# Four full-width partial sums moved from VectorE to accumulating DMAs, with the order of all steps rebuilt

## The chip, the cores and the metric

The kernel runs on one core of a Trainium2 chip. The time is the device time of one execution in microseconds (us), from the core's first instruction to its last, plus some 1.7 us that lie around the span which the profile shows (143.15 against 141.4 in the profiled run before). Every kernel is run several times, and the kernel before is run beside it on the same chip. Runs that lie over 1.5% above the fastest run of the same kernel are called slow and are left out of all comparisons.

## The reference, cut to what matters

Two independent halves work on 2048 positions of width 448 and are written side by side.

```python
def _A_ref(x, ...):                       # a state-space layer
    Bu = einsum("bld,pd->blp", x, B_bar)  # complex
    for t in range(L):
        h = Lam_bar * h + Bu[:, t, :]     # a scan over 2048 positions
    y = 2.0 * einsum("blp,dp->bld", hseq, Cmat).real + x * Dskip

def _B_ref(x, wqkv, wo):                  # local attention, 16 heads of 28
    q, k, v = ...                         # x @ wqkv
    idx = pos[:, None] - arange(8) * 2    # 8 keys per query, 2 apart
    attn = softmax(where(idx >= 0, q . k[idx] * scale, -1e9))
    o = sum over w of attn[..., w] * v[idx[..., w]]
    return o @ wo
```

The change concerns the sum over the eight window places `w` in half B. Half A shares all the engines with it.

## The kernel before

TensorE computes the projections, the scan of half A as matmuls over chunks, and the outputs. VectorE computes the eight products of the attention sum for each of four groups of four positions (a "quad": 0, 4, 8, 12), and most of the adds. (In the prediction and the expectations the quads are also counted from 0 to 3: "quad 2" there is quad 8 here, "quad 1" is quad 4.) Some adds are made by DMA: GpSimd issues a transfer from SBUF to SBUF that adds what it carries to what lies at its goal.

```python
def pv_m(self, j0, w):                    # step u.j.w: one product, on VectorE        (L325)
    ...
    self.nc.vector.tensor_tensor(self.pv_buf(j0, w), self.at[...]..., self.vd[...], op=ALU.mult)

def pv_a(self, j0, w, i0=0, i1=4):        # step d.j.w: accumulator += product w       (L330)
    acc = self.pv_buf(j0, 0)[:, i0:i1]
    self.nc.vector.tensor_tensor(acc, acc, self.pv_buf(j0, w)[:, i0:i1], op=ALU.add)

def pv_f(self, j0, w):                    # step f.j.w: product w += product w+1, DMA  (L334)
    a_, b_ = (self.pv_buf(j0, w + i)... for i in (0, 1))
    self.nc.gpsimd.dma_start(a_, b_, accum_op=ALU.add)
```

`pv_buf(j0, 0)` is the accumulator `pvb`, so `f.j.0` adds the product of w = 1 into the accumulator itself; the other products lie in `pvt`. Each such transfer carries 448 KB. A finished quad is turned by a transposing DMA (`tu`, oT<-pvb, L338) for the output product with `wo`. Half A loads its input by transposing DMAs and writes its output tile by tile:

```python
def load_x(self, a, b):                   # step X.a.b, two transposing DMAs           (L418, L419)
    self.nc.sync.dma_start_transpose(out=self.xT[:, b, 0:3, a, :], in_=...)
    self.nc.sync.dma_start_transpose(out=self.xT[:, b, 3, a, :], in_=...)

def y_e(self, a, b, eng):                 # step y.a.b: evict one output tile, store it
    ya = self.pool.tile([NCH, D], bf16, name="ya", tag="ya", bufs=3)
    self.cx.ev(eng, ya[:], self.ps_t["y", a, b][:])                 # PSUM to SBUF     (L83)
    self.nc.sync.dma_start(self.out_a[:, 4 * a + b, :], ya[:])      #                  (L717)
```

There are three tiles of `ya`: the fourth eviction must wait until the first store has landed. All transposing DMAs and stores are issued by SyncE (`SPq` in the page's list of issues), one after the other. The instruction order of every engine is fixed by one long table, read step by step: `L` local states of half A, `C`/`c` their corrections and evictions, `Y`/`y` half A's outputs, `O`/`o`/`od` half B's outputs, and so on; the last letter of an eviction, which copies a finished tile out of PSUM, where the matmuls write, names its engine (A ScalarE, V VectorE).

Of the kernel before, what the change touches and what calls it, by code (L numbers as in the profile page):

```python
# [16 lines left out]
S = 2048  # L17
D = 448
T = 16
# [4 lines left out]
H = 16  # L24
# [696 lines left out]
def body(ctx: ExitStack, tc: tile.TileContext, A_x, A_Lre, A_Lim, A_Bre, A_Bim, A_Cre, A_Cim, A_logdt, A_Dskip,  # L721
# [27 lines left out]


ORDER = """
    lw P.0.1.1.0.3 pp P.0.0.0.0.3 P.0.0.1.0.3 P.0.0.1.3.4 P.0.1.1.3.4 P.0.2.1 p.0.0.1.A p.0.1.1.A P.0.0.0.3.4 xa
    X.3.2 p.0.0.0.A P.0.1.0.0.3 P.0.1.0.3.4 p.0.2.1.A p.0.1.0.A P.0.2.0 p.0.2.0.A X.0.0 P.0.3.0 p.0.3.0.A
    P.1.1.1 p.1.1.1.A P.2.2.0 p.2.2.0.A P.2.1.1 p.2.1.1.A pe tb X.0.1 P.1.2.0 R.0.0.1.2 R.0.1.1.2 P.1.1.0
    p.1.1.0.A P.2.1.0 P.1.0.0 p.2.1.0.A tb tb p.1.2.0.A R.0.1.2.3 P.1.0.1 p.1.0.1.A P.1.3.0 p.1.3.0.A R.0.0.2.3
    R.0.0.0.1 S.0.0 T.0 St.0.0 R.0.1.0.1 S.0.1 St.0.1 s.0.A V.14 P.3.1.1 p.3.1.1.A p.1.0.0.A P.3.2.0 Z tb pg
    mt.0 mr.0 T.1 p.3.2.0.A sk mb.0.V P.1.2.1 p.1.2.1.A R.1.0 V.8 v.8.A X.1.1 P.2.0.1 P.2.2.1 p.2.0.1.A
    p.2.2.1.A V.9 v.9.A P.3.1.0 P.2.0.0 p.2.0.0.A p.3.1.0.A P.2.3.0 X.3.1 X.3.0 B.0 p.2.3.0.A X.2.0 P.3.0.1 ms.0
    X.1.0 me.0 B.6 R.1.1 S.1.0 St.1.0 b.6.A S.1.1 b.0.A St.1.1 P.3.0.0 p.3.0.0.A p.3.0.1.V B.3 V.13 X.1.3 b.3.A
    P.3.2.1 v.14.A s.1.A lc V.3 R.2.0 V.11 mt.1 p.3.2.1.A T.2 v.11.A R.2.1 B.1 mr.1 mb.1.A V.10 v.10.A S.2.0  # L760
    St.2.0 S.2.1 St.2.1 v.13.A s.2.A v.3.A X.2.2 V.15 P.3.3.0 R.3.0 p.3.3.0.A mt.2 V.5 V.0 R.3.1 v.15.A X.2.1
    V.2 ms.1 T.3 V.12 V.6 B.2 b.1.A v.0.A S.3.0 St.3.0 S.3.1 pa me.1 v.2.V v.12.A v.5.A St.3.1 s.3.A mr.2 mb.2.V
    X.1.2 ms.2 V.1 v.1.A v.6.A mt.3 M.1.V H.10.14 V.4 b.2.A V.7 M.2.V mr.3 me.2 mb.3.V M.4.V ms.3 M.0.V L.0.0
    B.4 M.3.V L.0.1 al me.3 l.0.0.A l.0.1.A N.0 n.0 L.0.3 l.0.3.A b.4.A X.2.3 v.7.A H.6.10 N.3 n.3 u.0.0 v.4.A
    B.5 L.1.1 l.1.1.A u.0.1 L.1.0 l.1.0.A N.15 n.15 b.5.A L.0.2 u.0.3 l.0.2.A X.0.2 L.1.3 L.2.6 l.2.6.A L.2.4
    u.0.2 L.2.2 l.2.4.A d.0.1 N.12 u.0.4 H.0.6 L.0.5 n.12 l.0.5.A L.2.1 l.2.1.A u.0.5 u.0.7 N.9 n.9 L.2.0 L.0.6
    l.1.3.A l.0.6.A l.2.0.A X.3.3 N.6 n.6 L.0.4 u.4.0 l.2.2.A l.0.4.A X.0.3 L.2.3 L.1.2 l.1.2.A L.3.2 f.0.2
    l.2.3.A L.3.3 l.3.2.A L.3.0 sa d.0.2 L.3.1 l.3.3.A l.3.0.A u.0.6 L.1.6 f.0.4 u.4.1 l.3.1.A sc la.0 L.1.4
    l.1.6.A u.4.2 u.4.3 d.4.1 d.0.4 L.1.5 le.0 ro.0 l.1.4.A u.4.5 l.1.5.A f.0.6 d.0.6 L.2.5 l.2.5.A L.3.6 sm
    sn.0 f.4.2 L.3.4 l.3.4.A bk.0 be.0.A u.4.4 f.4.4 d.4.2 l.3.6.A u.4.7 u.4.6 L.3.5 tu.0 G.2.A G.3.A l.3.5.A  # L770
    la.1 g.2.A g.3.A C.1.2.V C.0.2.V O.0.0 o.0.0.A C.1.3.A le.1 c.0.2.V ro.1 O.2.0 o.2.0.A c.1.2.V G.0.A c.1.3.A
    sn.1 f.4.6 u.8.0 C.2.2.A O.2.1 G.1.A bk.1 c.2.2.A g.0.A O.0.1 be.1.A G.5.V d.4.4 u.8.4 g.1.A G.4.V g.4.V
    C.0.1.A c.0.1.A Y.3.3 g.5.V o.0.1.A C.1.0.V d.4.6 tu.4 y.3.3.A c.1.0.V G.6.V g.6.V C.2.3.A c.2.3.A Y.1.3
    u.8.6 u.8.3 C.2.0.V C.0.0.A c.2.0.V u.8.7 Y.2.3 C.1.4.A Y.0.3 o.2.1.A od.2 f.8.6 u.8.2 od.0 c.0.0.A f.8.2
    c.1.4.A y.1.3.A C.2.4.V C.1.5.V y.2.3.A u.8.5 c.2.4.V c.1.5.V O.6.0 C.0.3.V c.0.3.V f.8.4 C.0.5.V O.6.1
    c.0.5.V y.0.3.A o.6.0.A C.0.4.A o.6.1.A od.6 u.8.1 C.0.6.V O.4.1 c.0.6.V C.1.1.V c.0.4.A c.1.1.V C.1.6.V
    O.4.0 C.2.5.V c.2.5.V d.8.1 Y.0.0 y.0.0.A C.2.1.V Y.2.0 Y.3.0 y.3.0.A c.2.1.V y.2.0.A o.4.0.A o.4.1.A od.4
    d.8.2 c.1.6.V C.2.6.V d.8.4 c.2.6.V u.12.2 Y.3.2 Y.2.2 d.8.6 u.12.4 Y.1.1 tu.8 Y.1.0 Y.0.1 y.2.2.A Y.1.2
    u.12.3 y.1.0.A y.0.1.A f.12.2 y.1.1.A O.8.0 o.8.0.A u.12.1 O.8.1 o.8.1.A Y.3.1 O.10.1 y.3.1.A u.12.5 Y.2.1
    u.12.6 f.12.4 y.1.2.A u.12.7 u.12.0 d.12.1 d.12.6 y.3.2.A O.10.0 o.10.0.A d.12.7 d.12.2 d.12.4.0.2 od.8  # L780
    tm.12 Y.0.2 o.10.1.A d.12.4.2.4 tm.14 te.12 O.12.0 O.12.1 od.10 y.0.2.A te.14 o.12.0.A o.12.1.A od.12
    y.2.1.A O.14.0 o.14.0.S O.14.1 o.14.1.S
"""


# [52 lines left out]
```

## Time and profile before

| | before |
|---|---|
| median time | 142.65 us (142.19 to 142.72, 3 runs) |
| TensorE busy | 134.3 us, 95% of the span of 141.4 |
| VectorE busy | 124.0 us, 88% |
| ScalarE, GpSimd busy | 57%, 32% |
| bytes on the queue that carries GpSimd's transfers | 6.65 MB, 26.2% of the time of 16 DMA engines |

The prediction shows the lines on TensorE and VectorE. Here are the DMA engines. The next lines are stretches of the trace of the kernel before: the stretch in us, its length, the busy time of TensorE, its weight loads, VectorE, ScalarE and GpSimd with their instructions, the granted TensorE clock as a share of full speed, the mean busy share of the 16 DMA engines (which goes above 1, here to 1.23), and GB/s.

```profile
66.00:72.00 6.00, 6.00 (x36) 3.18 (x35) 5.93 (x9) 3.38 (x7) 1.81 (x2) 1.00 0.78 134
72.00:78.00 6.00, 6.00 (x30) 2.68 (x29) 5.86 (x8) 3.42 (x7) 0.85 (x1) 1.00 1.23 188
...
84.00:90.00 6.00, 6.00 (x36) 3.12 (x35) 5.96 (x11) 4.54 (x11) 0.85 (x1) 1.00 0.51 96
...
114.00:120.00 6.00, 5.33 (x41) 2.95 (x39) 5.13 (x7) 1.92 (x5) 0.00 (x0) 1.00 0.44 147
120.00:124.00 4.00, 4.00 (x30) 2.25 (x27) 4.00 (x5) 0.99 (x2) 0.86 (x1) 1.00 0.78 158
```

From 66 to 90 us the DMA engines are full (a share of 1 or more) in one stretch of four (72 to 78); 78 to 84, left out, had a share of 0.84. From the list of DMA issues on the page (goal and source, issuer, how many, KB each, median us from issue to landing):

```profile
pvt<-pvt POOLq DMA_DIRECT2D x11, 448.0 KB, 4.7
out_dram<-ya SPq DMA_DIRECT2D x16, 112.0 KB, 3.8
```

### The profile page before, as it was taken

The numbers are of one execution on the slowest core, as the hardware profiler recorded it, in microseconds if no ns is written. First come the engines' busy times: TensorE is split into PE (matmuls) and PEld (weight loads), VectorE is DVE, ScalarE is ACT, GpSimd is POOL, SyncE is SP. The second block draws the span as 40 slices with busy tenths as digits, with TensorE's granted clock in tenths as the row PEclk, the third lists the DMA queues.
The fourth block names the chain that finished last, engine by engine and source line by source line (L and its number), as shares of the span: only waits on it lengthen the run. The fifth ranks groups of instructions, "written<-read, shape, count | busy, mean of one in ns | idle before, by whom it ended". The sixth has DMA issues, their size and how long they took to land. (4 is left out here: it accounts for less than half of the span.)

```text
span 141.4 us, 2554 instructions
## 1 busy us (share of the span) xinstructions
PE 134.3 (95%) x919; PEld 72.1 (51%) x919; DVE 124.0 (88%) x166; ACT 80.4 (57%) x166; POOL 45.0 (32%) x108
## 2 busy tenths in 40 slices
PE   6999999999998999999999999999999998999990
PEld 5244445555564756644544544655554554555540
DVE  0069999999999999999999999999999979999521
ACT  1238998759944947594465447555555123243680
POOL 8279599999940000002112200300024000220000
PEclk9999999999999999999999999999999999999998
DMA  4999898555762244526999956770379963797433
GB/s 108 292 202 197 188 221 112 104 115 114 156 151 49 52 101 121 135 56 175 143 163 196 188 96 130 133 131 0 74 218 214 205 172 130 163 212 178 151 111 134
DMA packets 36426, 20.49 MB, mean 145 GB/s; under 512 B 27762, under 2 KB 34048, under 8 KB 36413
## 3 DMA queue, kind: packets, MB, share of 16 engines
q1 hardware_dynamic: 33214, 13.32, 41.1%
q0 software_dynamic: 2736, 6.65, 26.2%
q10 hardware_dynamic: 463, 0.35, 1.0%
q8 instruction: 7, 0.11, 0.3%
q14 instruction: 6, 0.05, 0.1%
HBM read 3.62 MB, written 3.67 MB: 52 GB/s over the span
## 5 line engine op out<-in xcount | busy, mean ns | idle before, releaser
L325 DVE TENSOR_TENSOR pvt<-attn,vd 128x1792 bf16<-128x1792 bf16 x28 | 29.2, 1082 | 0.0
L600 PE MATMUL u_ps<-xaT,Bcat 128*128 128x512 bf16 x112 | 27.4, 379 | 0.0
L239 DVE TENSOR_TENSOR pr<-qT,kT 128x2048 bf16<-128x2048 bf16 (+1 forms) x12 | 26.9, 2279 | 0.0
L334 POOL DMA_DIRECT2D pvt<-pvt x11 | 9.5, 864 | 51.8 <-DVE pvt L325 51.5
L711 PE MATMUL y_ps<-C,u 128*128 128x448 bf16 x112 | 24.1, 353 | 0.7 <-DVE u L693 0.7
L83 ACT CAST u<-u_ps 128x512 bf16<-128x512 f32 x28 | 16.0, 591 | 12.8 <-PE u_ps L600 6.0
L191 PE MATMUL qk_ps<-xbT,wqkv_nat 128*128 128x512 bf16 x96 | 22.6, 382 | 0.0
L330 DVE TENSOR_TENSOR pvb<-pvb,pvt 128x1792 bf16<-128x1792 bf16 (+1 forms) x18 | 18.4, 1034 | 1.1 <-DMA pvt<-pvt 0.9
L83 ACT CAST ya<-y_ps 128x448 bf16<-128x448 f32 x16 | 8.1, 535 | 15.9 <-PE y_ps L711 11.2
L600 PEld LDWEIGHTS <-Bcat 128*128 128x128 bf16 x112 | 10.6, 98 | 11.2
L191 PEld LDWEIGHTS <-wqkv_nat 128*128 128x128 bf16 x96 | 9.2, 99 | 10.7 <-issue 1.0
L711 PEld LDWEIGHTS <-u 128*128 128x128 bf16 x112 | 9.8, 98 | 8.6 <-DVE u L693 1.1
L216 PE MATMUL v_ps<-wqkv_nat,xbT 128*128 128x448 bf16 x64 | 14.1, 355 | 0.0
L358 PE MATMUL wo_ps<-wo_p,oT 128*128 128x448 bf16 x64 | 14.1, 352 | 0.0
L83 ACT CAST kT<-qk_ps 128x512 bf16<-128x512 f32 (+3 forms) x22 | 9.9, 454 | 3.3 <-PE qk_ps L191 3.1
L83 ACT CAST qT<-qk_ps 128x512 bf16<-128x512 f32 (+1 forms) x20 | 9.4, 495 | 1.8 <-PE qk_ps L191 1.7
L83 ACT CAST yb<-wo_ps 128x448 bf16<-128x448 f32 x14 | 7.3, 537 | 5.4 <-PE wo_ps L358 5.3
L216 PEld LDWEIGHTS <-xbT 128*128 128x128 bf16 x64 | 8.6, 146 | 2.7 <-issue 0.2
L358 PEld LDWEIGHTS <-oT 128*128 128x128 bf16 x64 | 6.2, 98 | 5.9
L693 DVE TENSOR_TENSOR u<-co,u 128x512 bf16<-128x512 f32 x14 | 9.0, 678 | 0.0
L83 ACT CAST vd<-v_ps 128x448 bf16<-128x448 f32 x15 | 7.7, 541 | 1.6 <-PE v_ps L216 1.6
L577 POOL MEMSET Bcat<- 64x128 bf16 x7 | 1.4, 223 | 22.1 <-ACT Bcat L83 22.1
(177 smaller groups left out, 202.8 us busy)
## 6 DMA issues: line engine op xcount, KB each, us to landing
pvt<-pvt POOLq DMA_DIRECT2D x11, 448.0 KB, 4.7
out_dram<-ya SPq DMA_DIRECT2D x16, 112.0 KB, 3.8
out_dram<-yb SPq DMA_DIRECT2D x7, 224.0 KB, 2.2
vd<-vd SPq DMA_DIRECT2D x2, 392.0 KB
wqkv_nat<-in_B_wqkv_dram SPq DMA_DIRECT2D x2, 336.0 KB, 4.3
wo_p<-in_B_wo_dram POOLq DMA_DIRECT2D x16, 42.0 KB, 2.9
vd<-vd SPq DMA_DIRECT2D x1, 588.0 KB
xaT<-in_A_x_dram SPq DMA_TRANSPOSE x32, 3.5
```

The source lines that it names most:

```text
L83: nc.scalar.copy(out, in_)
L191: self.nc.tensor.matmul(self.ps_t[c, g, which][:], lhsT=wv[:, k], rhs=self.xT[:, k, c * CH:(c + 1) * CH], start=(k == 0), stop=(k == KT - 1))
L216: self.nc.tensor.matmul(ps[:], lhsT=xv[:, k, j, :], rhs=self.wn[:, k, 2, :], start=(k == 0), stop=(k == KT - 1))
L239: self.nc.vector.tensor_tensor(pr[:, :, g0:g1, :], self.qT[:, c, g0:g1].unsqueeze(1).to_broadcast([NCH, 4, n, CH]), self.windows(self.kT[: ...
L325: self.nc.vector.tensor_tensor(self.pv_buf(j0, w), self.at[:, w, j0:j0 + 4, :].unsqueeze(2).to_broadcast([NCH, 4, DH, H]), self.vd[:, off: ...
L330: self.nc.vector.tensor_tensor(acc, acc, self.pv_buf(j0, w)[:, i0:i1], op=ALU.add)
L334: self.nc.gpsimd.dma_start(a_, b_, accum_op=ALU.add)
L358: self.nc.tensor.matmul(ps[:], lhsT=oT[:, s + k, :], rhs=self.wo_p[:, KT * n + k, :], start=(k == 0), stop=(k == KT - 1))
L577: self.nc.gpsimd.memset(self.Bcat[0:PL, 3, i, :], 0.0)
L600: nc.tensor.matmul(ps4[:], lhsT=self.Bcat[:, k, m, :], rhs=self.xT[:, b, k], start=(k == 0), stop=(b % 2 == 0 and k == KT - 1))
L693: self.nc.vector.tensor_tensor(h_, ps, h_, op=ALU.add)
L711: nc.tensor.matmul(ps[:], lhsT=self.state(m, a, b), rhs=self.C[:, m, :], start=False, stop=(m == NM - 1), skip_group_check=True)
```

## The change

The intent is to relieve VectorE: in each of the four quads the add of the w = 1 product into the accumulator is done by a DMA, and the whole order is rebuilt around the new waits. No code but the order table differs. Its core, with the rest cut:

```diff
 ORDER = """
-    ... u.0.2 L.2.2 l.2.4.A d.0.1 N.12 u.0.4 H.0.6 ...
-    ... X.3.3 N.6 n.6 L.0.4 u.4.0 l.2.2.A l.0.4.A X.0.3 ...
-    ... l.3.1.A sc la.0 L.1.4 l.1.6.A u.4.2 u.4.3 d.4.1 d.0.4 ...
-    ... O.4.0 C.2.5.V c.2.5.V d.8.1 Y.0.0 y.0.0.A ...
-    ... f.12.4 y.1.2.A u.12.7 u.12.0 d.12.1 d.12.6 ...
+    ... L.0.0 l.0.5.A f.0.2 f.0.0 u.0.5 l.0.2.A L.1.4 L.1.3 l.1.4.A X.0.3 N.6 X.3.3 ...
+    ... d.0.6 L.1.6 l.3.2.A f.4.0 la.0 L.1.5 u.4.4 ...
+    ... f.8.2 tu.4 Y.0.3 u.8.1 f.8.0 C.0.0.V c.0.0.V C.0.4.V ...
+    ... Y.3.0 y.3.0.A y.1.0.A Y.2.0 f.12.0 u.12.3 f.12.2 Y.0.0 ...
     (all other steps: the same set in a new order, but for the engine that finishes 20 tiles:
      nine corrections, five group sums, six other evictions)
```

More of the change, by code (lines that the diff above doesn't have):

```diff
@@ L751 @@
 ORDER = """
-    lw P.0.1.1.0.3 pp P.0.0.0.0.3 P.0.0.1.0.3 P.0.0.1.3.4 P.0.1.1.3.4 P.0.2.1 p.0.0.1.A p.0.1.1.A P.0.0.0.3.4 xa
-    X.3.2 p.0.0.0.A P.0.1.0.0.3 P.0.1.0.3.4 p.0.2.1.A p.0.1.0.A P.0.2.0 p.0.2.0.A X.0.0 P.0.3.0 p.0.3.0.A
-    P.1.1.1 p.1.1.1.A P.2.2.0 p.2.2.0.A P.2.1.1 p.2.1.1.A pe tb X.0.1 P.1.2.0 R.0.0.1.2 R.0.1.1.2 P.1.1.0
-    p.1.1.0.A P.2.1.0 P.1.0.0 p.2.1.0.A tb tb p.1.2.0.A R.0.1.2.3 P.1.0.1 p.1.0.1.A P.1.3.0 p.1.3.0.A R.0.0.2.3
-    R.0.0.0.1 S.0.0 T.0 St.0.0 R.0.1.0.1 S.0.1 St.0.1 s.0.A V.14 P.3.1.1 p.3.1.1.A p.1.0.0.A P.3.2.0 Z tb pg
@@ L757 @@
-    mt.0 mr.0 T.1 p.3.2.0.A sk mb.0.V P.1.2.1 p.1.2.1.A R.1.0 V.8 v.8.A X.1.1 P.2.0.1 P.2.2.1 p.2.0.1.A
-    p.2.2.1.A V.9 v.9.A P.3.1.0 P.2.0.0 p.2.0.0.A p.3.1.0.A P.2.3.0 X.3.1 X.3.0 B.0 p.2.3.0.A X.2.0 P.3.0.1 ms.0
-    X.1.0 me.0 B.6 R.1.1 S.1.0 St.1.0 b.6.A S.1.1 b.0.A St.1.1 P.3.0.0 p.3.0.0.A p.3.0.1.V B.3 V.13 X.1.3 b.3.A
-    P.3.2.1 v.14.A s.1.A lc V.3 R.2.0 V.11 mt.1 p.3.2.1.A T.2 v.11.A R.2.1 B.1 mr.1 mb.1.A V.10 v.10.A S.2.0
-    St.2.0 S.2.1 St.2.1 v.13.A s.2.A v.3.A X.2.2 V.15 P.3.3.0 R.3.0 p.3.3.0.A mt.2 V.5 V.0 R.3.1 v.15.A X.2.1
@@ L762 @@
-    V.2 ms.1 T.3 V.12 V.6 B.2 b.1.A v.0.A S.3.0 St.3.0 S.3.1 pa me.1 v.2.V v.12.A v.5.A St.3.1 s.3.A mr.2 mb.2.V
-    X.1.2 ms.2 V.1 v.1.A v.6.A mt.3 M.1.V H.10.14 V.4 b.2.A V.7 M.2.V mr.3 me.2 mb.3.V M.4.V ms.3 M.0.V L.0.0
-    B.4 M.3.V L.0.1 al me.3 l.0.0.A l.0.1.A N.0 n.0 L.0.3 l.0.3.A b.4.A X.2.3 v.7.A H.6.10 N.3 n.3 u.0.0 v.4.A
-    B.5 L.1.1 l.1.1.A u.0.1 L.1.0 l.1.0.A N.15 n.15 b.5.A L.0.2 u.0.3 l.0.2.A X.0.2 L.1.3 L.2.6 l.2.6.A L.2.4
-    u.0.2 L.2.2 l.2.4.A d.0.1 N.12 u.0.4 H.0.6 L.0.5 n.12 l.0.5.A L.2.1 l.2.1.A u.0.5 u.0.7 N.9 n.9 L.2.0 L.0.6
@@ L767 @@
-    l.1.3.A l.0.6.A l.2.0.A X.3.3 N.6 n.6 L.0.4 u.4.0 l.2.2.A l.0.4.A X.0.3 L.2.3 L.1.2 l.1.2.A L.3.2 f.0.2
-    l.2.3.A L.3.3 l.3.2.A L.3.0 sa d.0.2 L.3.1 l.3.3.A l.3.0.A u.0.6 L.1.6 f.0.4 u.4.1 l.3.1.A sc la.0 L.1.4
-    l.1.6.A u.4.2 u.4.3 d.4.1 d.0.4 L.1.5 le.0 ro.0 l.1.4.A u.4.5 l.1.5.A f.0.6 d.0.6 L.2.5 l.2.5.A L.3.6 sm
-    sn.0 f.4.2 L.3.4 l.3.4.A bk.0 be.0.A u.4.4 f.4.4 d.4.2 l.3.6.A u.4.7 u.4.6 L.3.5 tu.0 G.2.A G.3.A l.3.5.A
-    la.1 g.2.A g.3.A C.1.2.V C.0.2.V O.0.0 o.0.0.A C.1.3.A le.1 c.0.2.V ro.1 O.2.0 o.2.0.A c.1.2.V G.0.A c.1.3.A
@@ L772 @@
-    sn.1 f.4.6 u.8.0 C.2.2.A O.2.1 G.1.A bk.1 c.2.2.A g.0.A O.0.1 be.1.A G.5.V d.4.4 u.8.4 g.1.A G.4.V g.4.V
-    C.0.1.A c.0.1.A Y.3.3 g.5.V o.0.1.A C.1.0.V d.4.6 tu.4 y.3.3.A c.1.0.V G.6.V g.6.V C.2.3.A c.2.3.A Y.1.3
-    u.8.6 u.8.3 C.2.0.V C.0.0.A c.2.0.V u.8.7 Y.2.3 C.1.4.A Y.0.3 o.2.1.A od.2 f.8.6 u.8.2 od.0 c.0.0.A f.8.2
-    c.1.4.A y.1.3.A C.2.4.V C.1.5.V y.2.3.A u.8.5 c.2.4.V c.1.5.V O.6.0 C.0.3.V c.0.3.V f.8.4 C.0.5.V O.6.1
-    c.0.5.V y.0.3.A o.6.0.A C.0.4.A o.6.1.A od.6 u.8.1 C.0.6.V O.4.1 c.0.6.V C.1.1.V c.0.4.A c.1.1.V C.1.6.V
@@ L777 @@
-    O.4.0 C.2.5.V c.2.5.V d.8.1 Y.0.0 y.0.0.A C.2.1.V Y.2.0 Y.3.0 y.3.0.A c.2.1.V y.2.0.A o.4.0.A o.4.1.A od.4
-    d.8.2 c.1.6.V C.2.6.V d.8.4 c.2.6.V u.12.2 Y.3.2 Y.2.2 d.8.6 u.12.4 Y.1.1 tu.8 Y.1.0 Y.0.1 y.2.2.A Y.1.2
-    u.12.3 y.1.0.A y.0.1.A f.12.2 y.1.1.A O.8.0 o.8.0.A u.12.1 O.8.1 o.8.1.A Y.3.1 O.10.1 y.3.1.A u.12.5 Y.2.1
-    u.12.6 f.12.4 y.1.2.A u.12.7 u.12.0 d.12.1 d.12.6 y.3.2.A O.10.0 o.10.0.A d.12.7 d.12.2 d.12.4.0.2 od.8
-    tm.12 Y.0.2 o.10.1.A d.12.4.2.4 tm.14 te.12 O.12.0 O.12.1 od.10 y.0.2.A te.14 o.12.0.A o.12.1.A od.12
@@ L782 @@
-    y.2.1.A O.14.0 o.14.0.S O.14.1 o.14.1.S
+    xa P.0.1.1.0.3 pp P.0.1.0.0.3 P.0.0.0.0.3 P.0.0.0.3.4 p.0.0.0.A P.0.1.0.3.4 P.0.1.1.3.4 p.0.1.0.A
+    P.0.0.1.0.3 X.2.3 X.3.2 P.0.2.0 p.0.1.1.A pe p.0.2.0.A P.0.0.1.3.4 P.1.1.0 X.3.1 P.0.2.1 X.1.0 p.1.1.0.A tb
+    P.1.2.0 X.3.0 p.0.0.1.V R.0.1.0.1 p.0.2.1.A R.0.0.0.1 R.0.0.2.3 P.2.0.1 R.0.0.1.2 p.2.0.1.A P.0.3.0
+    p.1.2.0.A P.1.0.1 p.0.3.0.A p.1.0.1.A X.2.2 P.1.1.1 p.1.1.1.A R.0.1.2.3 P.1.3.0 P.1.2.1 P.3.1.0 lc S.0.0 tb
+    T.0 St.0.0 p.1.2.1.A R.0.1.1.2 S.0.1 p.1.3.0.A St.0.1 s.0.A tb tb P.1.0.0 P.3.0.1 X.0.0 P.2.1.0 pg P.2.0.0
@@ new lines @@
+    p.1.0.0.A T.1 mt.0 mr.0 p.3.0.1.A mb.0.V X.0.2 p.2.0.0.A p.3.1.0.A lw R.1.0 p.2.1.0.A R.1.1 P.2.1.1 P.2.2.0
+    p.2.2.0.A P.2.3.0 p.2.3.0.A V.13 ms.0 B.1 P.2.2.1 p.2.1.1.A B.0 b.1.A p.2.2.1.A Z P.3.3.0 p.3.3.0.A P.3.2.1
+    p.3.2.1.A V.3 v.3.A B.6 b.6.A P.3.2.0 S.1.0 St.1.0 p.3.2.0.A b.0.A S.1.1 St.1.1 s.1.A v.13.A R.2.0 T.2
+    P.3.0.0 p.3.0.0.A V.9 R.2.1 v.9.A P.3.1.1 mt.1 X.2.0 me.0 V.12 v.12.A V.11 mr.1 X.2.1 B.4 p.3.1.1.A V.1
+    S.2.0 R.3.0 St.2.0 S.2.1 St.2.1 V.10 v.1.A mb.1.A ms.1 V.15 v.11.A T.3 V.8 R.3.1 v.15.A s.2.A V.14 mt.2 mr.2
@@ new lines @@
+    mb.2.V v.10.A M.1.V X.1.2 V.5 v.14.A me.1 b.4.A V.6 X.1.1 M.0.V V.7 v.8.A S.3.0 St.3.0 S.3.1 St.3.1 v.7.A
+    s.3.A v.6.A pa v.5.A sk ms.2 H.6.10 V.2 mt.3 me.2 V.4 v.4.A mr.3 mb.3.V v.2.A V.0 ms.3 al L.0.4 me.3 l.0.4.A
+    M.2.V M.3.V v.0.A B.3 N.3 N.0 n.3 B.2 L.2.1 L.2.0 b.3.A n.0 M.4.V H.10.14 u.0.3 L.2.3 l.2.1.A u.0.2 l.2.3.A
+    H.0.6 b.2.A N.12 L.0.3 l.2.0.A N.9 L.0.6 X.0.1 B.5 L.2.4 l.0.3.A L.0.2 b.5.A u.0.1 L.0.5 l.2.4.A u.0.0
+    l.0.6.A n.9 sm L.0.0 l.0.5.A f.0.2 f.0.0 u.0.5 l.0.2.A L.1.4 L.1.3 l.1.4.A X.0.3 N.6 X.3.3 l.1.3.A u.0.7
@@ new lines @@
+    X.1.3 u.0.6 L.1.2 l.0.0.A f.0.6 u.0.4 f.0.4 n.6 L.1.0 l.1.0.A L.0.1 u.8.0 L.2.2 u.4.3 L.3.3 d.0.2 l.2.2.A
+    l.0.1.A L.1.1 l.1.1.A L.3.1 u.4.1 l.3.1.A u.4.2 f.4.2 u.4.0 u.4.7 l.3.3.A l.1.2.A L.3.0 d.0.4 l.3.0.A L.3.2
+    d.0.6 L.1.6 l.3.2.A f.4.0 la.0 L.1.5 u.4.4 L.2.6 l.1.6.A L.2.5 N.15 l.2.6.A sa le.0 u.4.5 ro.0 L.3.6 u.4.6
+    f.4.6 L.3.4 l.2.5.A sn.0 bk.0 l.1.5.A l.3.4.A be.0.A u.8.3 n.12 l.3.6.A sc L.3.5 l.3.5.A G.1.V G.2.V g.1.V
+    n.15 d.4.2 tu.0 O.2.0 o.2.0.A la.1 le.1 g.2.V G.3.A g.3.A G.0.V O.0.0 g.0.V ro.1 sn.1 C.1.3.A f.4.4 C.1.2.A
@@ new lines @@
+    d.4.4 O.2.1 c.1.3.A C.2.3.A c.1.2.A o.2.1.A C.2.2.V c.2.2.V C.1.1.V c.1.1.V u.8.5 bk.1 c.2.3.A be.1.A Y.3.3
+    C.0.2.A c.0.2.A G.6.V G.5.A g.5.A g.6.V d.4.6 O.0.1 C.0.1.V G.4.A c.0.1.V u.8.2 C.1.6.A od.2 y.3.3.A g.4.A
+    f.8.2 tu.4 Y.0.3 u.8.1 f.8.0 C.0.0.V c.0.0.V C.0.4.V o.0.0.A c.1.6.A Y.1.3 c.0.4.V y.1.3.A u.8.4 f.8.4
+    y.0.3.A C.2.1.V u.8.6 Y.2.3 C.1.0.A C.0.6.V O.6.1 c.2.1.V o.0.1.A u.8.7 od.0 c.0.6.V C.0.3.V C.1.4.V c.1.4.V
+    C.1.5.V c.1.5.V u.12.0 O.6.0 d.8.2 f.8.6 y.2.3.A c.1.0.A Y.3.1 C.0.5.V c.0.5.V y.3.1.A Y.1.1 y.1.1.A Y.0.1
@@ new lines @@
+    y.0.1.A c.0.3.V Y.1.0 C.2.5.V u.12.1 C.2.6.V u.12.2 Y.3.0 y.3.0.A y.1.0.A Y.2.0 f.12.0 u.12.3 f.12.2 Y.0.0
+    c.2.5.V o.6.0.V C.2.0.V O.4.0 d.8.4 u.12.5 d.8.6 tu.8 u.12.4 f.12.4 o.6.1.A c.2.0.V od.6 C.2.4.V c.2.4.V
+    y.0.0.A o.4.0.A c.2.6.V O.4.1 u.12.6 d.12.6 Y.1.2 y.2.0.V u.12.7 Y.0.2 Y.2.2 O.10.0 o.4.1.A d.12.7 Y.3.2
+    od.4 d.12.2 d.12.4.0.2 y.0.2.A d.12.4.2.4 O.10.1 O.8.0 o.10.0.A o.10.1.A od.10 o.8.0.A tm.12 te.12 O.8.1
+    tm.14 o.8.1.A od.8 O.12.1 y.1.2.A O.12.0 y.2.2.A te.14 Y.2.1 o.12.0.A o.12.1.V y.3.2.A O.14.0 od.12 y.2.1.A
@@ L783 @@
+    o.14.0.S O.14.1 o.14.1.S
 """
```

## The prediction

> **What bounds the kernel now.** I read the page first (engine shares and slices), then the timelines of VectorE and TensorE, then the chain of waits that ended last, then the stretches with the DMA share.
>
> From the page: busy time, the slices, and the groups that the change touches (busy us, mean ns of one | idle before).
>
> ```profile
> PE 134.3 (95%) x919; PEld 72.1 (51%) x919; DVE 124.0 (88%) x166; ACT 80.4 (57%) x166; POOL 45.0 (32%) x108
> ...
> PE   6999999999998999999999999999999998999990
> ...
> DVE  0069999999999999999999999999999979999521
> ...
> L330 DVE TENSOR_TENSOR pvb<-pvb,pvt 128x1792 bf16<-128x1792 bf16 (+1 forms) x18 | 18.4, 1034 | 1.1 <-DMA pvt<-pvt 0.9
> ```
>
> VectorE has no gap between 8 us and 132.6 us but one. The reader would conclude that four adds fewer are four us less. But TensorE's row is as full, so a second bound stands close behind. From the timeline of TensorE (start, us, group, idle before):
>
> ```profile
> 35.48 0.83 PE L254 MATMUL lg<-pr,ones 128*32 128x512 bf16 x12 [0.21 <-DVE pr L239]
> ...
> 43.75 0.83 PE L254 MATMUL lg<-pr,ones 128*32 128x512 bf16 x12 [0.70 <-DVE pr L239]
> ...
> 117.96 0.36 PE L711 MATMUL y_ps<-C,u 128*128 128x448 bf16 x1 [0.67 <-DVE u L693]
> ...
> 134.45 3.21 PE L358 MATMUL wo_ps<-wo_p,oT 128*128 128x448 bf16 x16
> ```
>
> TensorE runs from 6.60 us (first projection) to 137.66 us, 131.1 us. How much of that is streaming? The last line: 16 matmuls of 448 columns in some 3.05 us from start to start, 190 ns each, 0.42 ns a column. Counting the columns of every step of the order by the loops of the kernel (a step's four logit sums share one pass, which took 0.64 us for twelve): Q/K projections 23.9 us, V 11.9, local states 28.4, logits 6.8, the y outputs 23.9, the wo outputs 11.9, corrections 6.0, the rest 10.8: 123.6 us. So 94% of TensorE's 131.1 us is unavoidable, 7.4 us is not. Of this the visible waits are 2.0 us: 0.21 + 0.70 + 0.19 + 0.19 in the logit stage (waiting for VectorE's products and maxima) and 0.67 at 117.96. The last really cost about 0.85: six matmuls from 115.99 end their issue at 117.11.
>
> The wait at 117.96 has its cause in the timeline of VectorE and in the chain of waits:
>
> ```profile
> 116.21 1.09 DVE L330 TENSOR_TENSOR pvb<-pvb,pvt 128x1792 bf16<-128x1792 bf16 x1 [0.86 <-DMA pvt<-pvt]
> 117.22 0.68 DVE L693 TENSOR_TENSOR u<-co,u 128x512 bf16<-128x512 f32 x1
> ```
> ```profile
> 107.06 9.06 DMA pvt<-pvt
> ```
>
> An accumulating DMA took 9.06 us to land, because three were issued from 105.05 to 107.9 beside two transposes and output stores. The add that needed it started 0.86 late, the correction behind it too, and TensorE stood. This is the price of a DMA add when several collide.
>
> [...] the trace has 1.00 us from start to start in a run (6.09 us for six multiplies), and 1.10 where each add needs the one before. [...] accumulating ones landed after 4.2, 4.7 (median) and 9.1 us at worst. [...]
>
> **The change part by part.**
> 1. Removed: in each of four quads the add of the w = 1 product into the accumulator, four full adds of L330: 4 x 1.00 = 4.0 us off VectorE. Added: four accumulating DMAs into the accumulator (11 become 15), on GpSimd 4 x 0.86 us, where it stands idle (32% busy). One f had to land before a later add in three places a quad, now the accumulator itself hangs on one.
> 2. Handed back to VectorE by the new order: one correction more (15 for 14, 0.60 from start to start), one group sum more (4 for 3, 0.47), the evictions of one y and two wo tiles (3 x 0.55); off it: one V eviction (0.55). A key eviction is swapped for another. Sum: -4.0 + 0.60 + 0.47 + 1.64 - 0.55 = -1.85 us in all. At the last add of the last quad, before one of those evictions, my running sum of VectorE's durations is 118.6 against 121.0: -2.4.
> 3. TensorE: an accumulation evicted by ScalarE needs an identity matmul first. One of 512 and one of 384 columns fall away: -0.37 us, 123.3 in place of 123.6. Nothing else changes in its work.
> 4. ScalarE (57%) and GpSimd have room. The DMA engines: before, the stretch 104 to 112 us moved 208 to 213 GB/s with a busy share of 0.78 to 1.08, and 122 to 127 again 1.07. Four more transfers of 448 KB fall in these stretches.
>
> On the path that sets the end: in the tail TensorE has, after the last add, two turns, one y and four wo outputs before (132.14 to 137.66, 5.5 us, no gap); in the new order two turns, five wo outputs and one y, 14336 columns or 6.0 us. So 0.75 us of work is moved behind the last add; 2.4 us on VectorE can become at most 1.7 there.
>
> With TensorE as bound: 0.37 us less work; the wait behind the DMA (0.85) goes if the order is well made; of the logit waits perhaps 0.4 to 0.6 (running sums of both engines: the last second-half products of chunks 1 to 3 come 0.5 us later, 0.1 earlier and 1.1 later on VectorE than before, but TensorE's needs move too, and the maximum of the last chunk, which gates all later work, comes 0.55 earlier). Together 1.6 to 1.8 at best. Against it: new waits. By the running sums, the second adds of quads 2 and 3 come only some 6 to 7 us after the issue of the DMA they need, with two or three more in flight; the transposed quad 2 has about 4.5 us from issue to its first use, where a transpose takes 4.0; the last y tile takes the buffer of a store issued some 3 us before, where a store takes 3.8. I take 0.5 for these, leaving -1.2 us.
>
> **The rivals.**
> (a) VectorE is the sole bound and the whole 1.85 to 2.4 us, perhaps with the 0.86 wait, comes off: 139.5 to 140.5. For it: VectorE's unbroken row. Against: TensorE's 123.6 us of columns in 131.1.
> (b) DMA contention takes it back: the 9.06 us landing happens in more places, VectorE waits some 1 us in two or three of the quads, TensorE behind it: 142.5 to 144. For: the busy share above 1.0 in two stretches. Against: before, 11 such DMAs gave one wait of 0.86, and the order was rebuilt with the new ones in it: the w = 1 transfers are issued 7 to 10 us ahead of their use.
> (c) TensorE alone, every wait staying: -0.37, 142.3.
> I hold a middle: TensorE binds, some of its waits go, new small ones come.
>
> **Range and chances.** 142.65 - 1.2 = 141.45. The range takes most of (a) at one end and a light (b) at the other: 140.2 to 142.8. Faster by over 2% needs 139.8, 2.85 us off: more than the 0.37 and all visible waits of TensorE (2.0) together; 0.07. Slower by over 2% needs several DMA waits on the path; 0.03.
>
> **What would show it.** VectorE busy about 122 us; L330 x14, L334 x15; TensorE idle before its matmuls still under 2 us and its first-to-last stretch about 130 us; the wait of 0.67 at the y outputs gone, smaller waits on pvt or pvb DMAs of 0 to 1 us in all; the last add ending at 129.5 to 130.5 us, but the last matmul only 1 to 1.5 us earlier than before. I am wrong if TensorE's stretch shrinks by over 2.5 us (then its 7.4 us of non-streaming time was slack after all), or if VectorE's waits for accumulating DMAs sum to over 2 us.

## The result

| | before | after |
|---|---|---|
| median time | 142.69 us (142.19 to 143.73, 4 runs) | 147.85 us (147.25 to 148.32, 4 runs) |
| ratio | | 1.035, 95% interval 1.028 to 1.042: slower |
| span in the profile | 141.4 us | 146.4 us |
| mean granted clock | 0.996 | 0.988 in all four runs |

All eight runs are fast ones. A ratio is the mean time of one kernel's fast runs over the mean of the other's of the same rounds, so it is not quite the ratio of the medians. The change costs 5.2 us where 1.2 us of gain were predicted.

The page after (busy time, slices, the group of adds, DMA issues):

```profile
PE 135.5 (93%) x907; PEld 72.6 (50%) x917; DVE 122.8 (84%) x166; ACT 78.6 (54%) x162; POOL 46.7 (32%) x112
...
PE   6999998999999999999949999999999949999990
...
DVE  0079999999999999999999399999998998399231
...
PEclk9999999999999999999999999999999986999999
...
L330 DVE TENSOR_TENSOR pvb<-pvb,pvt 128x1792 bf16<-128x1792 bf16 (+1 forms) x14 | 14.2, 1019 | 0.8 <-DMA pvb<-pvt 0.6
...
pvt<-pvt POOLq DMA_DIRECT2D x11, 448.0 KB, 5.2
pvb<-pvt POOLq DMA_DIRECT2D x4, 448.0 KB, 6.7
out_dram<-ya SPq DMA_DIRECT2D x16, 112.0 KB, 3.5
```

Four adds have left VectorE (18 to 14) and four transfers into `pvb` have come. VectorE is busy 1.2 us less, and that helped nothing: TensorE's row now has two 4s, in slices 21 and 33, and right after the second one the granted clock has a 6. VectorE's row has a 3 a little behind each of TensorE's gaps: it now waits for TensorE. From the timeline of VectorE:

```profile
113.38 1.09 DVE L330 TENSOR_TENSOR pvb<-pvb,pvt 128x1792 bf16<-128x1792 bf16 x1 [0.59 <-DMA pvb<-pvt]
...
126.46 0.69 DVE L693 TENSOR_TENSOR u<-co,u 128x512 bf16<-128x512 f32 x1 [2.65 <-PE co L685]
```

The first is all that VectorE waits for accumulating DMAs: 0.59 us, less than the 0.86 before. Now TensorE:

```profile
22.34 0.62 PE L254 MATMUL lg<-pr,ones 128*32 128x512 bf16 x8 [0.52 <-DVE pr L239]
...
73.86 0.82 PE L600 MATMUL u_ps<-xaT,Bcat 128*128 128x512 bf16 x3 [0.50 <-DMA xaT<-in_A_x_dram]
...
76.12 0.38 PE L600 MATMUL u_ps<-xaT,Bcat 128*128 128x512 bf16 x1 [1.44 <-DMA xaT<-in_A_x_dram]
...
115.88 1.49 PE L711 MATMUL y_ps<-C,u 128*128 128x448 bf16 x7
117.42 0.38 PE L685 MATMUL co<-u,mat 128*128 128x512 bf16 x1
119.83 0.53 PE L708 MATMUL y_ps<-Dg,xaT 128*128 128x128 bf16 x4 [2.03 <-ACT ya L83]
120.17 2.80 PE L711 MATMUL y_ps<-C,u 128*128 128x448 bf16 x7
```

The first of these lines is a new wait in the logit stage. The others show two stops. In the first, the local states of half A wait for input columns that a transposing load has not brought yet; before, no matmul waited for such a load. In the second, a y output waits 2.03 us for its PSUM bank, which ScalarE has not emptied. After the second, the same seven matmuls that took 1.49 us at 115.88 take 2.80 us. The timeline of ScalarE tells why the bank was full:

```profile
113.57 0.53 ACT L83 CAST ya<-y_ps 128x448 bf16<-128x448 f32 x1 [4.20 <-DMA out_dram<-ya]
...
119.24 0.53 ACT L83 CAST ya<-y_ps 128x448 bf16<-128x448 f32 x1 [4.30 <-DMA out_dram<-ya]
```

ScalarE waits twice for a y store to land so that one of the three `ya` tiles comes free, 8.5 us in all (before 1.5 us, once). The chain of waits of the kernel after names the transfers:

```profile
70.61 5.47 DMA xaT<-in_A_x_dram
...
109.70 9.44 DMA out_dram<-ya
...
119.24 0.54 ACT ya L83
...
119.83 0.53 PE y_ps L708 x4
120.36 2.61 PE y_ps L711 x7
```

The load at 70.61 us is the last of the x loads; SyncE issues the last eight transposes one behind the other from 58.41 us on. In the kernel before, the last was issued at 68.09 us, so part of the lateness lies in the issue, and not all in the 5.47 us to landing.

A store of 112 KB that lands after 3.5 us in the median took 9.44 us. The stretches show what lay beside it; compare them with those of the kernel before:

```profile
66.00:72.00 6.00, 6.00 (x32) 2.88 (x30) 5.93 (x8) 3.76 (x9) 2.37 (x3) 1.00 1.06 196
72.00:78.00 6.00, 4.01 (x18) 1.58 (x18) 6.00 (x7) 1.33 (x3) 1.00 (x2) 1.00 1.10 188
...
84.00:90.00 6.00, 5.95 (x29) 2.74 (x29) 5.95 (x11) 1.88 (x4) 1.71 (x2) 1.00 1.17 191
...
114.00:120.00 6.00, 3.92 (x28) 2.20 (x28) 6.00 (x9) 1.16 (x3) 1.72 (x2) 0.99 0.99 228
120.00:124.00 4.00, 4.00 (x20) 2.04 (x19) 3.81 (x4) 0.95 (x3) 0.00 (x0) 0.59 0.88 175
```

The DMA engines are full from 66 to 90 us (78 to 84, left out, has 1.09), where before they were full in one of the four stretches, and 114 to 120 has gone from 0.44 to 0.99. TensorE loses 2 us in 72 to 78 and 2 us in 114 to 120, and its granted clock falls to 0.59 in the stretch after. GpSimd had issued four accumulating transfers of quad 8 between 104.5 and 110.3 us, one of them the new one. By their bytes GpSimd's transfers make up queue q0 of the page (6.65 MB before, 8.49 with the four new ones) and SyncE's lie on q1 (13.32 MB in both kernels); beside the sums the store took 9.44 us all the same.

How the 5 us add up: for TensorE's matmuls I compared the actual start with the columns streamed up to there at about 0.42 ns each, the rate of the prediction's line of 16 matmuls (190 ns for 448 columns). The growth of the difference is what TensorE lost. Loss after minus loss before, in us: up to the local states 0.45; at the x wait 2.30; from there to the y wait -0.11; at the y wait 1.35 (2.2 in place of the 0.85 that the wait behind the late sum cost before); in the slow clock after it 1.70; in the rest -0.41. Together 5.3, less 0.37 for two smaller matmuls that fell away, 4.9: the last matmul ends at 142.6 us instead of 137.7.

### The profile page after: what moved, and what is told of

Same layout as the page of the kernel before. It is cut to its first block, busy times and chain, and to the rows that moved or that the text cites.

```text
span 146.4 us, 2545 instructions
## 1 busy us (share of the span) xinstructions
PE 135.5 (93%) x907; PEld 72.6 (50%) x917; DVE 122.8 (84%) x166; ACT 78.6 (54%) x162; POOL 46.7 (32%) x112
## 3 DMA queue, kind: packets, MB, share of 16 engines
q1 hardware_dynamic: 33214, 13.32, 43.0%
q0 software_dynamic: 3312, 8.49, 32.7%
## 4 chain that ended last, share of the span: by engine, by line
PE 52%; DVE 18%; DMA 10%; SPq 9%; ACT 6%; issue 3%; ACTq 0%; DVEq 0%
PE y_ps L711 11%; DVE pr L239 11%; PE wo_ps L358 7%; PE u_ps L600 7%; DMA out_dram<-ya 6%; SPq L418 5%; PE qk_ps L191 5%; DMA xaT<-in_A_x_dram 4%; PE v_ps L216 3%; SPq L419 3%; PE warm L68 3%; DVE prt L244 2%; PE y_ps L708 2%; ACT kT L83 2%; PE lg L254 2%
## 5 line engine op out<-in xcount | busy, mean ns | idle before, releaser
L711 PE MATMUL y_ps<-C,u 128*128 128x448 bf16 x112 | 25.2, 367 | 0.0
L83 ACT CAST u<-u_ps 128x512 bf16<-128x512 f32 x28 | 15.5, 590 | 15.3 <-PE u_ps L603 6.3
L330 DVE TENSOR_TENSOR pvb<-pvb,pvt 128x1792 bf16<-128x1792 bf16 (+1 forms) x14 | 14.2, 1019 | 0.8 <-DMA pvb<-pvt 0.6
L693 DVE TENSOR_TENSOR u<-co,u 128x512 bf16<-128x512 f32 x15 | 9.7, 682 | 2.9 <-PE co L685 2.9
L83 ACT CAST vd<-v_ps 128x448 bf16<-128x448 f32 x16 | 8.4, 538 | 2.6 <-PE v_ps L216 2.5
L83 ACT CAST yb<-wo_ps 128x448 bf16<-128x448 f32 x12 | 6.4, 536 | 5.6 <-PE wo_ps L358 3.6
L708 PE MATMUL y_ps<-Dg,xaT 128*128 128x128 bf16 x64 | 6.2, 222 | 2.0 <-ACT ya L83 2.0
```

The costliest lines, as they stand in the source:

```text
L83: nc.scalar.copy(out, in_)
L693: self.nc.vector.tensor_tensor(h_, ps, h_, op=ALU.add)
L708: nc.tensor.matmul(ps[:, KOFF[k] + c0:KOFF[k] + NCH], lhsT=self.xT[:, b, k, a, :], rhs=self.Dg[:, k, c0:], start=(k == 0), stop=False, ski ...
L711: nc.tensor.matmul(ps[:], lhsT=self.state(m, a, b), rhs=self.C[:, m, :], start=False, stop=(m == NM - 1), skip_group_check=True)
```

## The experiments

**Theory.** The added transfers take time of the 16 DMA engines, so transfers that TensorE needs come late: x loads in one place, y stores in another. VectorE's own waits play no part. **Rivals.** The rebuilt order is slow by itself; or the x loads are merely issued too late in it; or the slow clock is a cause of its own. Times are medians, and each run's ratio is to the kernel before on the same chip (142.9, 142.6 and 142.8 us there).

### All four sums back on VectorE, in the new order

```diff
-f.0.0  -f.4.0  -f.8.0  -f.12.0
+d.0.1  +d.4.1  +d.8.1  +d.12.1      (each in the same place of the new order)
```

> The changed kernel's order, with the four w = 1 adds back on VectorE at the places where the four accumulating DMAs were issued. Theory D (the four added DMAs slow the x transposes and the y stores): the waits of TensorE for the x transposes (0.5 + 1.4 us idle) and for the y tile (2.0) fall to under 0.7 together, the clock keeps to 1.0 between 120 and 124 us, and the time falls to 143 to 144.5. Theory O (the new order of loads, halos and stores makes the waits, whoever adds): the x wait stays above 1.2 us, at most the y wait shrinks, and with 4.0 us more on VectorE the time stays at 146.5 to 149.

Measured: 145.52 us (144.96 to 146.8), ratio 1.020 [1.012, 1.027]. The waits for x loads and y stores are gone, and no slice shows a lowered clock (mean 1.0 in the profiled run). TensorE comes to the step of the x wait at 73.2 us, in the kernel after at 73.4, so it is not TensorE that comes later: SyncE issues the last x load at 69.84 us instead of 70.61, and it lands in time. So the added transfers cause both stops. But the time is 1 us above the range of theory D, and the new order with VectorE adds is still 2.6 us slower than the kernel before: VectorE is busy 126.3 us and TensorE waits for it instead, most of all here:

```profile
88.92 0.38 PE L644 MATMUL bakA<-rt,ident 128*128 128x512 bf16 x1 [1.03 <-DVE rt L654]
```

In this order the relief of VectorE is needed; the transfers that give it cost more than it is worth.

### Two of the last four x loads, issued earlier

```diff
 ... l.2.3.A
+X.0.1 X.0.3
 H.0.6 ...          (and X.0.1, X.0.3 taken out at their later places)
```

The load that TensorE waited for is the last of the four, `X.1.3`; with these two out of its way SyncE can issue it sooner.

> The changed kernel with two of its last four x loads moved ahead of the last halo copy in SyncE's order, where SyncE stands idle from 53.9 to 57.0 us waiting for V evictions. Nothing else differs. Theory O: the wait of TensorE for x (idle 0.5 + 1.4, 2.3 us by column count) goes, time 147.8 - 2.3 = 145.5 (145 to 146). Rival (the DMA engines are too busy at 66 to 76 us, share above 1.0, so an earlier issue does not help): less than 0.8 us off, 147 to 148. A third way: the gain is eaten by the later y wait, which would then grow from 2.0 us.

Measured: one fast run, 144.42 us, and three slow ones, 147.43 to 164.18. The profile fell on a slow run, so neither its waits nor the median are used. One fast run 3.4 us below the kernel after hints that the x wait has its price, and no more: inconclusive. Why runs of one kernel differ by 20 us is not shown.

### Seven tiles for y instead of three

A pool of six plain `ya` tiles did not fit into SBUF: the build of the kernel after with it is refused, with 210.4 KB a partition asked for and 207.9 KB left. So the y tiles take turns with four tiles of the logit stage, which is over by then.

```diff
-ya = self.pool.tile([NCH, D], bf16, name="ya", tag="ya", bufs=3)
+i = self.ny = getattr(self, "ny", -1) + 1
+tag, bufs = (("ya", 3), ("ya", 3), ("ya", 3), ("lgb", 2), ("lgb", 2), ("mxb", 2), ("mxb", 2))[i % 7]
+ya = self.pool.tile([NCH, D], bf16, name="ya", tag=tag, bufs=bufs)
```

> The changed kernel with seven y tiles in SBUF for three (the four more lie in memory of tiles that are dead by then), so that ScalarE need not wait for a y store to land. Theory B (the buffer wait makes TensorE's gap, and the gap makes the clock drop): ScalarE's 8.5 us of waiting for y stores and TensorE's 2.0 go, the granted clock stays at 1.0 in 120 to 124 us, and the time falls by 2.2 + 1.7 = 3.9 to 144 (143.5 to 144.7). Rival (the stores hold up something else, or the clock drops by itself at that place): under 1.5 us off, 146.3 to 147.8.

Measured: 143.64 us (142.88 to 144.29), ratio 1.005 [0.999, 1.012], clock 1.0. That is 4.2 us less than the kernel after; the sum above gives the y wait and the slow clock 2.2 + 1.7 = 3.9. The stores themselves are no faster than in the kernel after:

```profile
out_dram<-ya SPq DMA_DIRECT2D x16, 112.0 KB, 4.8
```

They land after 4.8 us in the median (after: 3.5), but nobody stands behind them any more, and without the stop the clock is 1.00 from 120 to 124 us. An x wait of 0.89 + 0.27 us is left.

### Two of the sums by DMA in the old order

```diff
 (order of before)
-d.0.1  -d.4.1
+f.0.0  +f.4.0      (in the same places)
```

> The kernel before, with the w = 1 adds of quads 0 and 1 alone made accumulating DMAs, in place; the rest of the order stays. Theory T (TensorE binds, a DMA add by itself is harmless when issued well ahead): VectorE busy 2.0 us less, time 142.3 to 142.9. Rival V (VectorE is the bound): 140.7 to 141.5. Rival C (contention): a new wait on an accumulating DMA or a transpose, 143.3 to 145.

Measured: 144.28 us (144.03 to 144.41), ratio 1.009 [1.003, 1.016]. With the order untouched, two such transfers make TensorE wait for an x load, which it never did before:

```profile
75.40 0.38 PE L600 MATMUL u_ps<-xaT,Bcat 128*128 128x512 bf16 x1 [1.36 <-DMA xaT<-in_A_x_dram]
```

The wait of 1.36 us is about the whole loss, 144.28 - 142.9 = 1.4 us. VectorE had two adds less to do (1.03 us each in the mean of the page before), and nothing came of it. This speaks for the theory and against a fault of the new order alone.

### Useless matmuls in the gap

```diff
-C.2.6.V
+C.2.6.V wm          "wm": lambda: cx.warm(8, cols=CH)      (CH = 512)
```

> The changed kernel with eight useless matmuls of 512 columns (1.7 us) put into TensorE's order at the gap, between the last correction and the y output that waited 2.0 us; they write a PSUM tile that nobody reads. Theory G (the idle gap itself makes the granted clock drop for the next 3 us or so): the y outputs after it run at 1.5 us each as elsewhere, the clock stays at 1.0 in 120 to 124 us, and the kernel with more work is 1.4 to 1.7 us faster, 146.2. Rival (the clock drops there for another reason, such as the load before): the drop stays and the time is 147.8 to 148.5.

Measured: two fast runs, 145.18 and 145.44 us, ratio 1.019 [1.016, 1.021], and two slow ones. The fast runs are 2.5 us below the kernel after, although TensorE streams 8 x 512 columns more, 1.7 us at 0.42 ns a column. Their mean clocks are 0.995 and 0.999 (after: 0.988). This agrees with theory G, that a TensorE kept at work through the gap does not pay for it afterwards, but does not show it alone: the gain is 0.8 us more than the 1.7 us of the slow clock, and more than the 1.4 to 1.7 us expected. The profile fell on a slow run and is not used, so where the rest came from stays open.

### Only the sum of quad 8 back on VectorE

```diff
 (order of after)
-f.8.0
+d.8.1
```

> The changed kernel with one of the four added DMAs, that of quad 2 (issued at 105.5 us, among three others, two wo stores and four y stores), put back on VectorE. Theory D (this transfer is what makes the y stores late): the y store of 9.4 us lands in under 7, TensorE's wait of 2.0 falls under 0.8, the clock holds, and the time is 144 to 145; the x wait of 1.9 idle stays. Rival (it is the new order's burst of y stores, not the fourth transfer): the wait stays above 1.5 and the time above 146.8.

Measured: 143.94 us (143.62 to 144.7), ratio 1.010 [1.007, 1.013], clock 1.0. Taking back this one transfer of 448 KB gains 3.9 us, as much as the seven tiles. Now the stores do land earlier. Page and stretch of this run:

```profile
out_dram<-ya SPq DMA_DIRECT2D x16, 112.0 KB, 2.2
```
```profile
114.00:120.00 6.00, 5.95 (x45) 3.45 (x44) 6.00 (x8) 1.80 (x4) 1.72 (x2) 1.00 0.62 140
```

The median store takes 2.2 us instead of 3.5, the DMA share from 114 to 120 us is 0.62 instead of 0.99, and TensorE is busy 5.95 of 6 us instead of 3.92. The x wait (0.45 + 0.86 us) is left, as it must be.

### Only the sum of quad 0 back on VectorE

```diff
 (order of after)
-f.0.0
+d.0.1
```

> The changed kernel with the added DMA of quad 0 alone (issued at 65.8 us, in the middle of the last eight x transposes) put back on VectorE. Theory D: TensorE's wait for x (1.9 us idle, 2.3 by count) falls under 0.5, the y wait with its clock drop stays (3.9), time 145.2 to 146. Rival O (the place of the loads in SyncE's order makes the x wait): it stays above 1.2 us, time 147 to 148.

Measured: fast runs 148.02 and 149.47 us, ratio 1.043 [1.037, 1.049], and two slow ones. I had expected a gain, and it is a loss of about 1 us against the kernel after. The profile fell on a slow run. In it the x wait is gone, but that says nothing about the fast runs. The next experiment gives a fast profile with this sum on VectorE, though with seven tiles.

### Seven tiles and the sum of quad 0 on VectorE

> The changed kernel with seven y tiles and the quad 0 add on VectorE: both found waits attacked, three of the four added DMAs kept. If the x wait and the y wait are the whole loss, the time is that of the run with seven tiles (143.6) less the x wait left there (some 1.2 us): 141.8 to 142.6, at or just below the kernel before. If DMA contention costs at further places (the late wo inputs and stores), 143 to 144.

Its edit is the two edits above together. Measured: 146.04 us (145.12 to 146.89), ratio 1.026 [1.019, 1.032], 2.4 us above the seven tiles alone. My expectation missed. There is no wait for x loads and none for y stores, but two for the transposes of finished quads, which the kernel after does not have:

```profile
91.66 0.93 PE L358 MATMUL wo_ps<-wo_p,oT 128*128 128x448 bf16 x4 [1.79 <-DMA oT<-pvb]
...
129.68 0.93 PE L358 MATMUL wo_ps<-wo_p,oT 128*128 128x448 bf16 x4 [1.23 <-DMA oT<-pvb]
```

TensorE got to its first output sooner (at 89.87 us; in the kernel after, at 92.09) and found the input not yet there: its transpose took 10.9 us from issue to landing, against 6.8 in the kernel after and 9.0 with seven tiles alone. With the DMA engines full from 72 to 90 us (shares of 1.07 to 1.15 in this run), taking away one wait lets TensorE run into the next transfer. All its waits over 0.15 us come to 5.1 us here and to 2.8 with seven tiles alone, which is the whole difference of the two profiled runs (145.21 and 142.88 us). Why the transpose takes longer stays open.

### Seven tiles and the sum of quad 8 on VectorE

> The changed kernel with both cures of its second wait at once: seven tiles for y (alone 143.64 us) and the w = 1 sum of quad 2 on VectorE (alone 143.94). Theory W (both only take away the same wait of TensorE for a late y store, with the clock drop behind it): they do not add up; 143.3 to 144.2 us, and a wait for x columns of 1.0 to 1.5 us is left. Theory L (it is the load on the DMA engines as such, whoever waits for it): one transfer fewer is worth another 0.6 us or more on top of the tiles, 142.9 us or less.

The two cures of the y wait together. Measured: 143.56 us (143.41 to 144.44), ratio 1.007 [1.002, 1.013]. The cures do not add up (143.64 and 143.94 alone), so they take away the same wait. What is left is 1.51 us of TensorE waiting for an x load at 75.3 us.

### Seven tiles in the kernel before, as a control

> Control: the kernel before with seven tiles for y, nothing else. ScalarE waited there for a y store once, 1.5 us, and TensorE's wait of 0.67 behind a late sum had another cause. Theory W: no wait of TensorE is taken away, 142.3 to 142.9 us, the same as before. Rival (the tiles are worth something in any order, so that the seven-tile runs overstate what the added transfers did): 141.5 us or less.

Measured: 142.42 us (141.92 to 143.6), ratio 0.999 [0.993, 1.005]. The tiles are worth nothing where no late store holds up TensorE, so the 4.2 us above are no general gain. None of the kernels tried beats the kernel before.

### The sum of quad 8 alone by DMA, in the old order

```diff
 (order of before)
-d.8.1
 u.8.1
+f.8.0
```

> The kernel before with the w = 1 sum of quad 2 alone by an accumulating DMA, issued right after its product, and nothing else changed. Theory L (the stretch from 104 to 112 us has no room, a share of 0.78 to 1.08 already): the y stores and the other sums of quad 2 land later, TensorE waits 1 to 2 us more than before, 143.5 to 145 us. Rival (only the new order brings y stores and sums together): 142.2 to 142.9 us, no new wait of TensorE.

Measured: 149.17 us (148.32 to 149.28), ratio 1.043 [1.037, 1.049], clock 0.971 to 0.988. The direction is right, the size is three times what I expected, and the way is another. From the timelines of TensorE and of VectorE, and the stretches:

```profile
120.43 0.59 PE L685 MATMUL co<-u,mat 128*128 128x512 bf16 x1 [5.23 <-DVE u L693]
...
121.20 2.80 PE L711 MATMUL y_ps<-C,u 128*128 128x448 bf16 x7
```
```profile
118.68 1.09 DVE L330 TENSOR_TENSOR pvb<-pvb,pvt 128x1792 bf16<-128x1792 bf16 x1 [5.80 <-DMA pvb<-pvt]
```
```profile
120.00:124.00 4.00, 3.57 (x14) 1.74 (x14) 4.00 (x6) 0.00 (x0) 0.00 (x0) 0.50 0.00 0
```

Here it is VectorE that stands, 5.80 us, for the new transfer into the accumulator, which took 8.70 us from issue to landing by the chain of waits; behind VectorE's correction TensorE stands 5.23 us, and then runs at a granted clock of 0.50. One such transfer in the wrong place costs 6.3 us. The rebuilt order does what it was made for: it gives VectorE other work for that time, so that the same four transfers cost VectorE 0.59 us. But the transfers into the accumulator still take long there (6.7 us in the median), and the next in need of the DMA engines was the y store.

## Why the prediction was wrong

- **Which engine binds: right.** VectorE lost 1.2 us of work (predicted 1.85) with 14 adds and 15 transfers as predicted, and the time did not follow. TensorE binds, and its stops decide.
- **The waits named as gains: half right.** The 0.67 us behind the late sum is gone. Of the logit stage's waits, 1.29 us before, 1.16 are left (0.52 + 0.31 + 0.33), where I had put 0.4 to 0.6 us as gained: the one of 0.52 us is new and falls on the products of chunk 0, while I had followed chunks 1 to 3. TensorE even comes 0.45 us later out of that part as a whole; why is open. The first three projection matmuls, which took longer (1.11 us instead of 1.05), are worth 0.07 us of it at most.
- **VectorE's waits for accumulating DMAs, 0 to 1 us: right, 0.59.** This is the trap. Both signs that I had named as proof of error (a TensorE stretch shorter by over 2.5 us, VectorE waiting over 2 us) stayed silent while the prediction was off by 6.4 us. The forecasts beside them did fail: TensorE's waits came to 5.1 us where under 2 was said, and its stretch to 136.0 us where it was 130.
- **The failed step is part 4, the DMA engines, with "I take 0.5 for these".** I wrote down that four more transfers would fall into stretches with a share near 1, and then priced only those who read what the transfers write. I did list the transposed quad and the last y tile as tight; it was a middle y tile, whose store took 9.44 us where I had put 3.8, and the x loads, which I had not looked at because no matmul had waited for one. In place of 0.5: the x wait 2.3, the y wait 2.2, both by the column count. The runs bear out the second: without it 4.2 or 3.9 us come back, together with the clock. The x wait was not isolated: in the runs without it (all sums on VectorE, or quad 0's) other waits stood in its place.
- **A term that was missing: the clock.** A stop of 2.03 us was followed by seven matmuls in 2.80 us instead of 1.49, at a granted clock of 0.59 from 120 to 124 us: 1.7 us lost. No term of my sum allowed a wait to cost more than its length. Not every stop does: after one of 1.79 us, in the run with seven tiles and quad 0's sum on VectorE, four wo matmuls took 0.93 us (elsewhere in that run 0.92), and the mean clock of that run is 1.0. What decides is not shown.
- **Rival (b), contention: right in kind, wrong in its carrier and its size.** I had it arrive at VectorE and make 142.5 to 144. It arrived at TensorE by way of SyncE's loads and stores, at 147.85. My argument against it, that 11 such transfers gave one wait of 0.86, counted waits and not room: two added to the old order already cost 1.4 us, and quad 8's alone 6.3.
- **The last add** ended at 135.8 us instead of 129.5 to 130.5, because VectorE, for which I had computed its own running sum, was held up twice by TensorE's stops (2.21 and 2.65 us).
- **A small slip.** No transpose flew with the three transfers of 105.05 to 107.9 us, as the prediction says of two: the last one before had landed at 104.1 us.

What stays open: why returning quad 0's sum to VectorE made the kernel slower and, with seven tiles, a later transpose so slow; what the transfers of quads 4 and 12 cost (neither was taken back alone); what decides whether the granted clock falls after a stop of TensorE; and why some of these orders have slow runs in half of their executions and others none.

## What to carry to other kernels

Before work is handed to a DMA, look in the stretches where it will fly for the DMA share, and price the delay of every other transfer there, above all stores whose tiles are reused after three and loads that the bounding engine reads. Here the x wait cost 2.3 us and the y wait 2.2, and the wait of VectorE, which reads the results, 0.59. TensorE had no slack, and relieving VectorE of 1.2 us of work gained nothing. A stop of 2.03 us on TensorE lost another 1.7 us through a granted clock of 0.59; after one of 1.79 us in another run the clock did not fall. The y wait fell on the return of a buffer, and more buffers (143.64 us), one transfer fewer (143.94) and both at once (143.56) were cures for the same wait that did not add up.
